# A conformer layer on one core: a table in the source sets the order of each engine's work

## The chip, the cores and the metric

The kernel runs on one core of one Trainium2 chip. The metric is the device time of one execution in microseconds. Five engines work side by side, each through its own queue of instructions in order: PE (TensorE), ACT (ScalarE), DVE (VectorE), POOL (GpSimd) and SP (SyncE, here for transfers). They wait for one another by semaphores alone.

## The reference

Two sequences of 4000 tokens, 144 features, 4 heads of 36. All data is bfloat16.

```python
h = _layernorm(x);  h = _silu(h @ w_ff1a) @ w_ff1b;  x = x + 0.5 * h
q, k, v = heads(_layernorm(x) @ w_qkv)
p = softmax(q @ k.T * Dh ** -0.5);  x = x + (p @ v) @ w_o
h = _layernorm(x) @ w_pw1;  h = h[..., :D] * _sigmoid(h[..., D:])
c = depthwise_conv(h, dw)                 # 5 taps along the tokens
x = x + _silu(c) @ w_pw2
h = _layernorm(x);  h = _silu(h @ w_ff2a) @ w_ff2b;  x = x + 0.5 * h
return _layernorm(x)
```

The hidden width of the feed-forward parts is 576. The scores are 4000 x 4000 for each head and sequence; they are the bulk of the work.

## The kernel before, in words

The tokens are cut into 16 chunks of 500 (`CH`), eight for each sequence. The keys are cut into tiles of 64 (`KT_ROWS`), 62 whole ones and one of 32. One step of attention takes one chunk of queries and one tile of keys, all four heads:

- *Scores*: four matmuls of 64 x 64 tiles on PE write two PSUM banks (PS<-QT,KT in the profile).
- *Exp*: one ACT instruction over both banks, 128 x 1000, gives the probabilities (PT<-PS). One step in about six has its exp on DVE instead: five instructions that build it from bit patterns (`dve_tile`).
- *Values*: four matmuls (PS<-PT,VA) add probabilities times values into two banks that are kept for a whole chunk.

Six PSUM banks go round among scores and everything else. The everything else is the work of a chunk before its attention (`ff1`, `pre2`: layer norm, transposes, feed-forward with tanh on ACT, projections) and after it (`epilogue`, `post1`, `post2`: division, output projection, gated convolution, second feed-forward, store). It is woven into the attention steps. In the loop a layer norm takes its statistics on DVE (ST<-X) and the rest on POOL (RS and XN), then eight transposes on PE and a copy on DVE.

No loop of the chip's program stands in the source. A planner runs when the kernel is built. `Rec.op` records each instruction with the tiles that it reads (`r`) and writes (`w`), and gives it a planned start and end from costs in the source, among them 0.095 us when PE changes from one kind of matmul to another (`SWITCH`). `Sched` holds one thread for each piece of work and `pick` takes the next piece by planned times, tables of settings for stretches of 21 steps (`POLICY`) and hand-set offsets. The order in which pieces are recorded is the order in which each engine gets them. `Rec.finish` then derives the waits: for each instruction, the latest one on every other queue that it depends on, unless an earlier wait covers it. `replay` writes the instructions out, all at one line, so that all rows of the profile carry that line; the tiles tell them apart.

In the same engine a write after a read or after a write needs no wait in this kernel (`not raw` in `finish`), because the queue is in order; a read after a write does, but on PE.

Of the kernel before, what the change touches and what calls it, by code (L numbers as in the profile page):

```python
# [44 lines left out]


class Op:
    __slots__ = ("eng", "name", "a", "k", "idx", "deps", "clock", "inc", "waits", "cnt", "q", "done", "t0", "t1", "kind")


class Rec:
# [4 lines left out]
    LAT = dict(pe=0.165, act=0.12, dve=0.083, pool=0.1, sp=2.0)  # L56
    SEM = dict(pe=0.053, dve=0.036, act=0.045, pool=0.08, sp=0.1)
    SWITCH = 0.095

    def __init__(self, nc):  # L60
        self.nc = nc
        self.ops = []
        self.n = {}
        self.hist = {}
        self.free = {e: 1.0 for e in self.ENGS}
        self.kind = None
        self.last = 0.0
        self.filler = None
        self.filling = False

    def op(self, eng, name, *a, r=(), w=(), q=None, cost=0.1, kind=None, lat=None, **k):
        o = Op()
        o.eng, o.name, o.a, o.k, o.q = eng, name, a, k, q
        o.deps, o.inc, o.cnt = [], False, 0
        lane = eng if q is None else "q:" + q
        for key in r:
            h = self.hist.setdefault(key, ([], []))
            o.deps += [(d, True) for d in h[0]]
            h[1].append(o)
        for key in w:  # L80
            h = self.hist.setdefault(key, ([], []))
# [24 lines left out]
        o.t0, o.kind = start, kind  # L106
        o.done = start + cost + ((self.LAT[eng] if q is None else 2.0) if lat is None else lat)
        self.last = o.done
        self.ops.append(o)
        return o  # L110

    def ready(self, key, eng):
        h = self.hist.get(key)
        return max([o.done for o in h[0]], default=0.0) + self.SEM[eng] if h else 0.0

    def finish(self, group_qs=()):
        eng_clock = {e: {} for e in self.ENGS}
        for o in self.ops:
            clk = eng_clock[o.eng]
            need = {}  # L120
            for d, raw in o.deps:
                lane = d.eng if d.q is None else "q:" + d.q
                if d.q is None and d.eng == o.eng and (d.eng == "pe" or not raw):
                    continue
                if clk.get(lane, -1) >= d.idx:
                    continue
                if lane not in need or need[lane].idx < d.idx:
                    need[lane] = d
            keep = []
            for lane, d in need.items():  # L130
                if any(l2 != lane and d2.clock.get(lane, -1) >= d.idx for l2, d2 in need.items()):
                    continue
                keep.append((lane, d))
            new = dict(clk)
            for lane, d in keep:
                d.inc = True
                for l2, v in d.clock.items():
                    if new.get(l2, -1) < v:
                        new[l2] = v
                if new.get(lane, -1) < d.idx:  # L140
                    new[lane] = d.idx
            o.waits = keep
            eng_clock[o.eng] = new
            o.clock = new
        self.sems = {}
        cnt = {}
        for o in self.ops:
            lane = o.eng if o.q is None else "q:" + o.q
            if o.q is not None:
                cnt[lane] = cnt.get(lane, 0) + 16  # L150
                o.inc = True
            elif o.inc:
# [87 lines left out]
class Req:  # L240
    __slots__ = ("eng", "slots", "kids", "cond", "dur", "kind", "hold")
# [17 lines left out]
class Sched:  # L259
# [26 lines left out]
        return kids  # L286

    def advance(self, th, item):
        self.cur = th
        n0 = len(self.R.ops)  # L290
        self.stepped = False
        try:
            th.req = th.gen.send(item)
        except StopIteration:
            th.live = False
            self.threads.remove(th)
        new = self.R.ops[n0:]
        if new:
            th.ready = max(th.ready, max(o.done for o in new))
# [24 lines left out]
def bass_standalone__conformer_family_zipformer__speech_kernel(  # L324
# [24 lines left out]
    R = Rec(nc)  # L349
# [165 lines left out]
    RD = sb("RD", [2, NB, 2], F32)  # L515
    AN = sb("AN", [NAN, NB, D])
# [765 lines left out]
    SAVE = QT[:, 1, T:T + 4 * CH * NQ].bitcast(F32).rearrange("p (c k n) -> p c k n", c=NQ, k=2)  # L1282
# [338 lines left out]
    while n_s[0] < NIT or eq or pend or live_dve[0]:  # L1621
        seg[0] = max(seg[0], n_s[0] // SEG)
        if mode["front"] and len(kv_done) == CPB:
            mode["front"] = False
            front[:] = [0.0, n_s[0]]
            S.add(setup_dw())
            for par in range(NPRE):
                S.add(series(pre(c) for c in range(CPB + par, NCH, NPRE)), R.last)
            for par in range(2):
                S.add(series(post2(c) for c in range(par, NCH - ALONE, 2)), R.last, rank=2)  # L1630
            for c in range(NCH - ALONE, NCH):
                S.add(post2(c), R.last, rank=2 if c < NCH - 1 else -1)
# [33 lines left out]
    while S.threads:  # L1666
        c = [(S.start_of(th), th) for th in S.threads]
# [38 lines left out]
```

## Time and profile before

| | before |
|---|---|
| median of 3 runs | 914.98 us (914.81 to 915.06) |
| profiled execution | 914.9 us, its span 913.1 us |
| granted clock | 0.999 |
| PE, matmul | 890.1 us busy, 11946 instructions |
| ACT | 872.9 us busy, 1105 |
| DVE | 802.0 us busy, 1756 |
| POOL | 277.5 us busy, 519 |

A busy time is the union of an engine's instructions from start to end. The ends of matmuls are modelled, and neighbours on ACT overlap, so a busy time is no measure of how tightly an engine's instructions follow one another. The chain of work that ended last is followed back from the end: at each step to what released the instruction, or to the one before it on its engine. "PEld" is PE's loading of weights, which runs beside its matmuls.

### The profile page before, as it was taken

How to read it: one execution, taken by the hardware profiler on the slowest of the kernel's cores; microseconds unless marked ns; L12 is line 12 of the kernel's file. 1: busy time of each engine (PE TensorE's matmuls, PEld its weight loads, DVE VectorE, ACT ScalarE, POOL GpSimd, SP SyncE). 2: the span in 40 equal slices, each digit the busy share in tenths (PEclk: the TensorE clock that was granted, in tenths of full speed). 3: DMA queues.
4: the chain of work that ended last, by engine and by line, in shares of the span. 5: the costliest groups of instructions: out<-in, count | busy, mean ns of one | idle time of the engine just before them, and what ended most of it. 6: DMA issues, size and time to landing. Idle time of an engine off the chain costs nothing.

```text
span 913.1 us, 27439 instructions
## 1 busy us (share of the span) xinstructions
PE 890.1 (97%) x11946; PEld 411.2 (45%) x11946; DVE 802.0 (88%) x1756; ACT 872.9 (96%) x1105; POOL 277.5 (30%) x519
## 2 busy tenths in 40 slices
PE   8999999999999999999999999999999999999996
PEld 7544434444444444444444444444434344444455
DVE  8988898898989999898988799897889699978987
ACT  5899999999999999999999999999999999999984
POOL 5121041145111612223415333240605050403143
PEclk9999999999999999999999999999999999999999
DMA  4000000000000000000000000000000000000000
GB/s 114 34 2 1 2 2 1 1 3 1 3 3 1 3 2 2 2 3 1 2 2 14 1 9 8 8 2 1 15 1 2 8 9 2 8 1 8 2 8 26
DMA packets 7322, 7.36 MB, mean 8 GB/s; under 512 B 2376, under 2 KB 7202, under 8 KB 7202
## 3 DMA queue, kind: packets, MB, share of 16 engines
q1 hardware_dynamic: 5786, 5.00, 1.8%
q8 instruction: 93, 1.52, 0.7%
q10 hardware_dynamic: 1416, 0.62, 0.3%
q14 instruction: 27, 0.22, 0.1%
HBM read 3.31 MB, written 2.30 MB: 6 GB/s over the span
## 4 chain that ended last, share of the span: by engine, by line
ACT 51%; PE 43%; DVE 4%; issue 1%; DMA 0%; POOL 0%; POOLq 0%; DVEq 0%
ACT PT L170 46%; PE PS L170 43%; ACT TH L170 5%; DVE HT L170 1%; DVE PT L170 1%; DVE ST L170 1%; DMA X<-in_x_dram 0%; DVE X L170 0%; DVE XN L170 0%; DVE QT L170 0%; POOL RS L170 0%; DVE XT L170 0%; DVE RS L170 0%; DVE SW L170 0%; DVE VA L170 0%
## 5 line engine op out<-in xcount | busy, mean ns | idle before, releaser
L170 ACT ACTIVATE PT<-PS 128x1000 bf16<-128x1000 f32 (+1 forms) x841 | 777.2, 1050 | 8.3 <-PE PS L170 5.9
L170 PE MATMUL PS<-QT,KT 64*64 64x500 bf16 x3968 | 415.6, 383 | 8.6 <-ACT PT L170 5.6
L170 PE MATMUL PS<-PT,VA 64*37 64x500 bf16 x4636 | 396.1, 373 | 1.9 <-DVE QT L170 1.4
L170 DVE TENSOR_SCALAR PT<-PS 128x500 int16<-128x500 f32 x334 | 222.4, 671 | 31.5 <-PE PS L170 29.5
L170 PEld LDWEIGHTS PS<-QT,KT 64*64 64x64 bf16 x3968 | 123.8, 104 | 195.7 <-ACT PT L170 112.5
L170 PEld LDWEIGHTS PS<-PT,VA 64*37 64x37 bf16 x4636 | 132.1, 95 | 111.3 <-issue 26.7
L170 POOL TENSOR_SCALAR RS<-ST 125x4 f32<-125x4 f32 x112 | 36.6, 327 | 471.0 <-DVE ST L170 465.8
L170 DVE TENSOR_SCALAR PT<-PT 128x1000 uint16<-128x1000 uint16 x334 | 134.7, 416 | 1.3
L170 POOL TENSOR_SCALAR XN<-X,RS 125x144 bf16<-125x144 bf16 x224 | 131.8, 599 | 5.8
L170 POOL TENSOR_TENSOR RS<-RS,NHALF 125x4 f32<-125x4 f32 (+2 forms) x101 | 94.1, 936 | 101.6 <-DVE RS L170 96.9
L170 DVE TENSOR_TENSOR PT<-PT 128x1000 bf16<-128x1000 bf16 x167 | 113.0, 681 | 1.5
L170 ACT ACTIVATE TH<-PS 128x500 bf16<-128x500 f32 (+3 forms) x198 | 104.3, 552 | 6.7 <-PE PS L170 5.6
L170 DVE SCALAR_TENSOR_TENSOR HT<-TH,PS 128x500 bf16<-128x500 bf16 (+1 forms) x135 | 80.6, 616 | 25.1 <-ACT TH L170 24.4
L170 PE MATMUL PS<-XT,WA 72*128 72x500 bf16 (+2 forms) x280 | 74.3, 360 | 0.6 <-DVE VA L170 0.3
L170 DVE SCALAR_TENSOR_TENSOR X<-PS,X 125x288 bf16<-125x288 f32 x128 | 57.4, 452 | 14.8 <-PE PS L170 13.1
L170 DVE BATCH_NORM_STATS2 ST<-X 125x6 f32<-125x288 bf16 (+1 forms) x160 | 65.8, 447 | 1.0 <-DMA X<-in_x_dram 0.8
L170 PE MATMUL PS<-WB,HT 128*125 128x144 bf16 (+1 forms) x640 | 52.7, 230 | 0.3 <-DVE HT L170 0.3
L170 PEld LDWEIGHTS PS<-WB,HT 128*125 128x125 bf16 (+1 forms) x640 | 44.3, 136 | 14.8 <-issue 3.8
L170 PE MATMUL PS<-IDENT,XN 125*72 125x125 bf16 x512 | 42.4, 221 | 1.5 <-DVE XN L170 0.9
L170 DVE COPY XT<-PS 72x1000 bf16<-72x1000 bf16 (+2 forms) x65 | 39.9, 617 | 3.3 <-PE PS L170 2.5
L170 PEld LDWEIGHTS PS<-IDENT,XN 125*72 125x72 bf16 x512 | 31.5, 112 | 20.2 <-issue 12.6
L170 PE MATMUL PS<-U,DG 128*128 128x250 bf16 (+5 forms) x204 | 34.3, 265 | 0.1
(86 smaller groups left out, 560.6 us busy)
## 6 DMA issues: line engine op xcount, KB each, us to landing
X<-in_x_dram SPq DMA_DIRECT2D x16, 140.6 KB
out_dram<-XN SPq DMA_DIRECT2D x14, 140.6 KB
WA<-in_w_ff1a_dram ACTq DMA_DIRECT2D x1, 144.0 KB
WB<-in_w_ff1b_dram ACTq DMA_DIRECT2D x1, 144.0 KB, 2.6
WA<-in_w_ff2a_dram SPq DMA_DIRECT2D x1, 144.0 KB
WB<-in_w_ff2b_dram SPq DMA_DIRECT2D x1, 144.0 KB
out_dram<-XN SPq DMA_DIRECT2D x2, 70.3 KB
WQKV<-in_w_qkv_dram ACTq DMA_DIRECT2D x1, 121.5 KB
```

Of the source, the lines that this page charges most:

```text
L170: ins = getattr(eng, o.name)(*o.a, **o.k)
```

## The change

The planner runs as before and records the same instructions with the same tiles, buffers and costs. Each recorded instruction now also carries a step number, `step`, which goes up by one with every piece that the planner takes. The instructions of one engine with one step number are a block. After planning, `reorder` permutes the blocks of each engine by a table in the source: one letter for each block, P for a block that stays, other letters for so many places forward or back. Then it lays the five queues into one list that respects every dependency, numbers the instructions anew, and `finish` derives the waits from that.

The dependencies get a third state. A hazard within one engine (a write after a read on the tiles in `LATE`, or with a memset) is marked `None`; `finish` skips only those marked `False`, so it may now wait for its own engine there.

```diff
+ALPHABET = '!#$%&()*+,-./0123456789:;<=>?@ABCDEFGHIJKLMNOPQRSTUVWXYZ[]^_`abcdefghijklmnopqrstuvwxyz{|}~'
+ORDER = {
+    "pe": (
+        "PPPPPPQOPPPPPPPQOPPPQQQQLPPPPQOPRPNRPNQQNPPPWOfNNNcMQMPMINPNLNNOMOMNNPTPNOOPPPPRPNPPROORRUMMPNRTMNRO"
...
+    "act": (
+        "PPPPPPPPPPPQRNOPPPPPPPPQOPPPPPPPPPROQNPPPPQOPPPPPPQOPQOPPPPRORNOPPPPPPPPPPPPPPPPPQQNPPPQOQOPPPPPPPPP"
...
+    "sp": (
+        "PPPPPPPQOPRPN"
+    ),
+}
...
+    LATE = ("MV", "RS", "NM", "VE", "RD", "AN", "XN", "SAVE")
...
         for key in w:
             h = self.hist.setdefault(key, ([], []))
-            o.deps += [(d, False) for d in h[0] + h[1] if d is not o]
+            late = key[0] in self.LATE
+            for d in h[0] + h[1]:
+                if d is not o:
+                    hazard = late and d in h[1] or "memset" in (name, d.name)
+                    o.deps.append((d, None if hazard else False))
...
+    def reorder(self, table):
+        lines = {}
+        for e in self.ENGS:
+            blocks = {}
+            for o in self.ops:
+                if o.eng == e:
+                    blocks.setdefault(o.step, []).append(o)
+            shift = [ALPHABET.index(c) - 45 for c in table[e]]
+            blocks = list(blocks.values())
+            shift += [0] * (len(blocks) - len(shift))
+            at = [None] * len(blocks)
+            for i, blk in enumerate(blocks):
+                assert at[i + shift[i]] is None
+                at[i + shift[i]] = blk
+            lines[e] = [o for blk in at for o in blk]
+        out, seen, pos = [], set(), {e: 0 for e in self.ENGS}
...
-                if d.q is None and d.eng == o.eng and (d.eng == "pe" or not raw):
+                if d.q is None and d.eng == o.eng and (d.eng == "pe" or raw is False):
                     continue
...
     def advance(self, th, item):
+        self.R.step += 1
...
         t, k, v = pick()
+        R.step += 1
...
     R.stats = stats
+    R.reorder(ORDER)
     R.finish(group_qs=("w0", "w1", "w2", "w3"))
```

More of the change, by code (lines that the diff above doesn't have):

```diff
@@ L32 @@
 EXP_BIAS = 127.0 * 128 - 76.4453125
+ALPHABET = '!#$%&()*+,-./0123456789:;<=>?@ABCDEFGHIJKLMNOPQRSTUVWXYZ[]^_`abcdefghijklmnopqrstuvwxyz{|}~'
+ORDER = {
+    "pe": (
+        "PPPPPPQOPPPPPPPQOPPPQQQQLPPPPQOPRPNRPNQQNPPPWOfNNNcMQMPMINPNLNNOMOMNNPTPNOOPPPPRPNPPROORRUMMPNRTMNRO"
+        "RPRPRRGRMOQRSQSQYIPY[GPZR[IR[GRZRY[SABBQVRUU?AEFTKPRRLMPPQRROUQJNOOPPSOPQMPPPPPPPPPQRRMNPPQSPMQNQOSO"
+        "ORNOPPPPPQQNROOPQOPSPNRNOQOPPPPPPPPPPPPPPPPPPPPPPPPPPTOPNOQOTOPNVNOVNPMMOOPQOTOPSMPMQOPPQOPQOPPPPPPP"
+        "PPPROOTOTPMMRNTPMORRMWPLUPVLOVQUHQHVQITQIMMPPPPPRORPMPQOPPPRRNNQOPRTQNLOPQQNPRPNQQNRPRPUPJOOOPQRNOQQ"
+        "NQQRMQNPPUPNSVMMUPKMNQQMQOPSPNRNOQOTOSPMMQOQQNPQQNPSOOOPPPPPPPPPQQNPQOPQQNROOPPPPPPQOQOPPSOOOPPPPPPP"
+        "PPPQOPROOSSNNRMTNOORNTNOORNTRMNSMPNSOPNTOPNQQQLQRNOQRNTNUNOSLNNQQRRLQMQQQMQOQOPPPUOPPPLQXNOOPPPPKPRS"
+        "QMRLRNQSMORNWNPPQLPRTKPRSKRSSJRURISTISPSTHTHSPSJRSSHSQJRRSIRSKPSKSNSMNRNVPQQKRRRRIRJRRRLRRRJRRKRMRRM"
+        "RM[QMPQXKOOOJXNLQQQKTTTINKRRSJRXKQQQJXOJPQLVOLPQLUMTOORRJQSPIQNQUNPPRLNSSNSMMOSSNNSPLQRMQRMQRRLQRLRR"
+        "MQRRRJWRPJPUKTMULMMSOMQRRLSPLQRRLSPLRRMSPLRRRLWQKPPQKUPLPRRLSQRJQRKSPMQRMSPMQQRLSQMQVLPPQUKRLOMPPQOR"
+        "SSSMKMPQQNUOOOOOWOOOOPPMUVNNNOMRNOQRNOQSPPLPPPPQQNQOPSOOQQMPPQOPPPPPPPPPPPPPPPPQOPPPPQQNPPPPQQQMQOPP"
+        "PPPPROOROQNPPPPPPRPNPPPPPPPPPPPPPPPPPPPQOPPPPPPQOPQOPPPQOPPPPQOPPTOOOOPPSOOOPPQOPPQOPQOPSPNRPRPTQINO"
+        "PPPPPPROQUMOOPNSOORPMRPNQOPRPNQQQMPPQQNPSOOQNPQOPQOPQOPSSNNNPQOPSSNNNQQNROOQQQMQQNPQOPQQQMRPNPRRN[MO"
+        "PPMYNNNNVNLNOMVNPPPLVNUPULOKLQNQRNQRMUWMNNNNPQTLPRMQTLOPRMQSMORRMQQLPQORRNNPQQQSLOOPQOROOPROOPPQOQQN"
+        "QQQMQRNOROOSOOQNQOQQQMQQNQQRMQQMQOQQQMQQQMQSNOQRMRNQQMPQRSOLQRMQQRLQQQLRPQMRPNROOQQNROOROOQOUOTQMMMQ"
+        "RNRPMQQNPQQNROOPQQNPQQNROOPQOROOPPPPQQNPPQTNOPNRPRMOPQQNPPQQNQOQQNQQQQLROOQOQQQMQOQQQMQQQMQOPQQRMQNR"
+        "PNQORPNQQNQQQMSQRNRKOPQQNROOPQQSSLRNLQOQQNQQNQQSMOQNRPSMRNNSOOZNOOOOPPMRXNLPNTUPLLLQNPQOQQNROORPNQOQ"
+        "QQQQKQQQMPPRPQQQKQQNROQNPPPPPPPPPPPPQOQOPPPPPPPPPPQOPPPPPPPQOPPQOPQOPPPQOQOROOSOOSNOQNQOQQQMPPROOPPP"
+        "PPQQNPPSOOOPQOPPPPPPQSNOOPQOPPPQQQMRPNPPXQNNOOPNOPTQNNOXOOOPNOORNQQSLPNQQNPPPPQQQMPQQNPQOPPPPPPQOPPP"
+        "QQNRPUPPSJNNPQOPPPPPPPPPPPUOQNNQQQLQQNPPPPPPPPQQSPLOQOPRPNPQOTOPNOQOPPROQSMORNOPQOQOQOPQQNPPPQOQOQOP"
+        "QQNPQOQQNQOQOQQNQQQMROOQQNQQQMSPNOQOSOOOQOPPQOPPPQOPPPQQQQQKRSQMMPROOPQRRMNPSSNNNPPPPRRRRSQRRRGGPPPP"
+        "PPPPPPPPQQNPPPPPPPPPPPPPPPPPSOOOPPQOPPQOPPQOPPPPTPNOOQOQOPQQNPPQOPPPPPPPPPPPPPPPPPPPPPPPPPPPQQQQLQOP"
+        "PPQOROOPQOPPQORPNQOPPQOQOPQQQRLQRMQQMPQOPROOQQNPQQNRPNPPPPSOOOPPQOPPQOPRPNQORPNQQNRPNQOPPQOPPSOOOPPP"
+        "PPPPQOPPQOPQQNPSSNNNQQQMQQRMQQMQOQQNROOPPPQQQMPQVNOUNNNRMNPSPPQLQQNRPNSOPSSSNJVPPJUNNTMNRMNZPPPLPNRP"
+        "MMPPPSPNOPSOPNSPNOQOPQOQOQOPROOQQNPQTNOOOPQRNQQRLQRMQQMQQRMQNQQSMRNNPRRRRUKQJRMRRLQMRRORLOPQOPQQNPQQ"
+        "QMPPPPPPQOQQRMOPPPPRRNNPQORROMQQRMRNOQQQQLROOQQQMPPPPPPPROOPPQOPQOPPQOPQOPPQOPPQQNPQOSOOOPROOPPPQOQQ"
+        "NPPPQQNPPPPPPPPPPQOPPPPPPPPPPPPPPQOPPPQOPQQNPPPQQNUOOOOOQOQOROOQOPPPRPQQLPPPQOPQOPQQNPPQOPPPQOPTOOOO"
+        "SOOTNOOZNPXMNOULPLLLQQNRPRMOROOPVOOOOOOROQNPROQSMPRMQNQOPPPPPQOPPPPPQOPPPPPPPPRPNPQQNROOPPPPPPQQNQOP"
+        "PPPPPPPPPQOPPSSNNSMROMQQQMPPPPPPPPPPPQOQTNPNQNPQRNQRRLSMPQRRSJRRKSPKQQRLQQMQOPQQNSSNNNPQOPQOPQOPVOWN"
+        "QULQSSISQGIQQNVOSUSTKKTJJSSSSSMIRHOPQQNPROOQOQRPMPQSPPLQOSPNOROOPPPSOPNPPROOPROOPPPPPQQN"
+    ),
+    "act": (
+        "PPPPPPPPPPPQRNOPPPPPPPPQOPPPPPPPPPROQNPPPPQOPPPPPPQOPQOPPPPRORNOPPPPPPPPPPPPPPPPPQQNPPPQOQOPPPPPPPPP"
+        "PPPPPPPQOPPPPQOPPPPPPPPPPPPPPPPPPPPPPPPPPPPPPPPPPPPPPPPPPPPPPPPPPPPPQOPPPPPPPPQOPQOPPQOPQOPPPPPPPPPP"
+        "PPPPPPPPPPPPPPPPPPPPPPPPPPPPPPPPPPPPPPPPPPQOPPPPQOPROOPSOOOPPPPPPPPPPPSSNNSMOOPPPPPPRSNNOPPPPPPPPPPP"
+        "PPPPPPPPPPRRNNQQNPPPPPPPPPPPPPPPPPPPPPPPPPPPPPPPPPPPPPPROOPPPPPPPPPROOROOPPQOQOPPPPPPPPPPPPPPPPPPPPP"
+        "PPPPPPPPPPPPPPPPPPPPPPPPPPPPPPPQOPPPROOPPPPPPPPPPPPPPPPPPPPPPQOPPPPPPPPPPPPPPPPPPPPPPQOPPPPPPPPPPPPP"
+        "PPPPPPPQOPPPPPPPPPQQNPPQOPPPPPPPPPPQOPPPPPPPPPPPPPQOPPQOQOPPPPQOPPPPPPPQOPPPPPPPQOPPQOPPPPPPPPPPPROO"
+        "PPQQNPPPPPQOPPPQOPPQOPPPPPPPPPPPPPPPPPPPPPPPPPPPPPPPPPPPPPPPPPPPPPROOPPPPPPPPPPPPPPPPPPPPPPPQOPPPPPP"
+        "PPPPPPPPPPPPPPPPPPPPPQOPPPPPPPPQOPPQOPPPPPQQNPPPPPQOPPPQOPPPPPQOPPPPPPPPPPPPPPPPPPPPPPPPPPPPPPPPPPPP"
+        "PPPPPPPPPPPQOPPPPPPPPPPQOPPPPPPPPPPPPPPPPPPPPPPPPPPPPPPPPPPRPNPPPQRNOPPPPPTOOOOPQOPPPPPPPPPPPPPPPPPP"
+        "PQOPQOPPPPPPPPPPQOPPPPPPPPPPPPPPPPPPPPPPPPPPPPPPPPPPPPPPPPPPPROOPQOPPPPPQOPPQOPPPPPPPQOPPPQOPPPPPPPP"
+        "PPPPPPPPPPPPPPPPPPPPPPQOPPPPPPPPPPPPPROOROOPQOPPPPPPPPPPPPPPPPPPQQNPPQQQMPPQOPPQOQQQQQQJPQO"
+    ),
+    "dve": (
+        "PPQOPPQOPPPROOcOOOR`MMMNQMMMPMMZOMTPPHUQRLTRPWRBOTEOMNPSOOOQOPQQQSQKQMWRPNLOOOPPPPPTOOOQNPPPVPPQQTQQ"
+        "TTFPGRRRNQRGQNPUPRUNKMXNYMOQOKOQJNPPR[NNOYNZMMMMMMQQKRKRNOPQOPPPQOQQNPQOQSNOOPQOPPPPPPPPPPPPPPPQRRRR"
+        "KRKQNRPNPTPPPTPTOOSOPQRPQQQQQQQQSPSS5RSQRTJSSESSKRJ^PPJOOOOOOOQNNQOPQOPPPPPROQNQOPPPPPPQOQOQOPPTRSMR"
+        "LQKPPPPPQQNQOPPPPPPPPPPPPPQOPPPPPPPPPPQOQOQOPQOSQNNRVNNPN`NNOOOPNZNNNNNNNNOOQOPPPPQQQMPQOROSNRNQMPPP"
+        "PPPPPPQQNPPPPPPPPPSPNOROOQOPPPPPPPSOOOPTPPSLPSPKSNORNORPNSPNSNOSNROMPPPPPRPNROOQOROQQMQOPQOQORPNROOR"
+        "OQQQLPPPQOPPQOPQOPSOPNQOPQQNPQOPPPPPRPSMPNROORPNPRPNQOQQN[OPNQNNPNOPNPPPROOPPPQOPPPPPPPPPPPPPPPPPPPP"
+        "PPPPPPPQOPPPPPPPPPPQOPPPQOPPPPPPPPPPPPQQNPPPPPPQOQRPSPKOPPPPPQOPQOPPPPPPPQOPPPQOQOQOPPPPPPPPPQQNPPQO"
+        "PPUOOOTOTLNNRNOSOPSPLRNQNPPPPQRNOPPPPPPPPPPPPPPPPPPPPPRRRMQQKPSOTOMOQNPPPPPPPPPPROQNPQOPPPQOPPPPPPPP"
+        "PPYOOOOOOOOORTRMMNPPPPPPPPPPQOQOPPPPPPPPPQOQOPQQRMQQQQQQSHPQMPPQOPQQQMPQQNROUNOOOOPQOPPPPPPPPQOUOPNO"
+        "OPTOQRMMPPPPPPPPPPPPPPPPPPPPPPPPPPPPVPQMPPLPQQQMPPPPPPQOPPQOPPPPPPQOPPPPQOPPPPPPPQOQOPQOPSPNRNOQQNQR"
+        "NOPSOPNoOOOOOOOOOOOOOOOOOOOOOPNOOOPNPNQOPPPPPPPPQOPROOROOSPROQKPPPPPPPPPPRPRMQQQQKPPQOPQQNPPPPPPPPPP"
+        "PPPQOPPPPPPPPPPPPPQQNPPQOPPP_OOOOROQLPLPNPNPWORNNNPNPPPPPPQOPPPPPPPPSORORLOPPQORPNPQOPQQQMQOPPPPPPPQ"
+        "QQMPPPQOPQOQRNQNPQOPPPPPPPQOQOPPQQQRPKPPQQNPQQNPRPQMPPPPPPPPPPQOPPPPPROQNPRPNROOQOPQOQQNPQOPQORPQQLR"
+        "RNQMPPSPNOPPTPNPQQLQQNPPPPPPPPPPPPPPQOQOPPPPQOPPPQOPPPPQOQOPPPPPPQOUOPNRNQMPPROOPPPPPPPPPPPPPPPPPPPQ"
+        "QRPQQQIPPROOPROQNQOPPPQQNPPQOPPPPPPPPPPPPROQNPRPQMQOPPPPPPPPPPPPPPPPPPQOPQOPPPPQQQMPRORPRPKPPPPPPPPR"
+        "OQQQLPPRPNPPPPPPPPPPPPPQOPPPPP^ROSLPLPLOOOOOROOQTTPLMNPQOPQRTOPROISOOOWPQORPNQHQOPTOSOTLMOORPNQOPQOP"
+        "PPPPPPPPPQQQM"
+    ),
+    "pool": (
+        "PQQQRPQQRPQSQOQQQQQQRPQQQRPQQQQQQQQQRPQQQRP%QOYOOOOOOSNORPQQIPPSQNQMPQZUQQKLSTJSKTKUUNNOFQUPQJNOPPTR"
+        "NVMMOWPNPKORNQMPRPQMPPPPPQO"
+    ),
+    "sp": (
+        "PPPPPPPQOPRPN"
+    ),
+}
@@ L47 @@
 class Op:
-    __slots__ = ("eng", "name", "a", "k", "idx", "deps", "clock", "inc", "waits", "cnt", "q", "done", "t0", "t1", "kind")
+    __slots__ = ("eng", "name", "a", "k", "idx", "deps", "clock", "inc", "waits", "cnt", "q", "done", "t0", "t1", "kind", "step")
 class Rec:
@@ L68, in __init__ @@
         self.filler = None
+        self.step = 0
         self.filling = False
@@ L105, in op @@
         self.free[eng] = o.t1 = start + cost
-        o.t0, o.kind = start, kind
+        o.t0, o.kind, o.step = start, kind, self.step
         o.done = start + cost + ((self.LAT[eng] if q is None else 2.0) if lat is None else lat)
@@ L114, in ready @@
         return max([o.done for o in h[0]], default=0.0) + self.SEM[eng] if h else 0.0
+    def reorder(self, table):
[14 more added lines that the diff above has]
+        out, seen, pos = [], set(), {e: 0 for e in self.ENGS}
+        while len(out) < len(self.ops):
+            n = len(out)
+            for e in self.ENGS:
+                while pos[e] < len(lines[e]):
+                    o = lines[e][pos[e]]
+                    if any(id(d) not in seen for d, raw in o.deps):
+                        break
+                    seen.add(id(o))
+                    out.append(o)
+                    pos[e] += 1
+            assert len(out) > n
+        count = {}
+        for o in out:
+            lane = o.eng if o.q is None else "q:" + o.q
+            o.idx = count.get(lane, 0)
+            count[lane] = o.idx + 1
+        self.ops = out
     def finish(self, group_qs=()):
```

## The prediction

> **What bounds the kernel now.** The page comes first: the span, the busy shares and the chain that ended last.
>
> ```profile
> span 913.1 us, 27439 instructions
> PE 890.1 (97%) x11946; PEld 411.2 (45%) x11946; DVE 802.0 (88%) x1756; ACT 872.9 (96%) x1105; POOL 277.5 (30%) x519
> ACT 51%; PE 43%; DVE 4%; issue 1%; DMA 0%; POOL 0%; POOLq 0%; DVEq 0%
> ```
>
> ACT and PE hand the chain to each other; nothing else carries it. The profiled execution took 914.9 us, 1.8 us outside its span, and the median of the runs is 914.98 us, so the sum below is made against 914.9. The windows view then splits the span into front, attention loop and tail. Its columns are PE, PEld, DVE, ACT and POOL busy, the granted clock and the DMA.
>
> ```profile
> 0.00:60.00 60.00, 56.04 (x674) 35.19 (x675) 53.83 (x169) 44.54 (x76) 20.93 (x42) 1.00 0.20 57
> 60.00:870.00 810.00, 798.42 (x10852) 350.50 (x10851) 715.72 (x1484) 801.92 (x982) 238.22 (x447) 1.00 0.01 4
> 870.00:913.10 43.10, 35.59 (x428) 25.50 (x423) 32.48 (x105) 26.41 (x49) 18.35 (x31) 0.97 0.06 18
> ```
>
> In the loop ACT shows only 810.00 - 801.92 = 8.1 us idle. That number is too small, and the reason decides this case. Two stretches of the chain and the groups of ACT in the loop show it:
>
> ```profile
> 771.31 23.09 ACT PT L170 x26
> 513.91 0.96 ACT TH L170 x2
> ...
> L170 ACT ACTIVATE PT<-PS 128x1000 bf16<-128x1000 f32 x800 | 745.1, 1058 | 6.6 <-PE PS L170 4.2
> L170 ACT ACTIVATE TH<-PS 128x500 bf16<-128x500 f32 x116 | 71.4, 642 | 0.5 <-PE PS L170 0.2
> L170 ACT ACTIVATE TH<-PS 128x250 bf16<-128x250 f32 x22 | 10.3, 470 | 0.5 <-PE PS L170 0.5
> L170 ACT ACTIVATE PT<-PS 128x500 bf16<-128x500 f32 x15 | 10.0, 669 | 0.0
> L170 ACT ACTIVATE TH<-PS 64x125 bf16<-64x125 f32 x15 | 4.1, 275 | 0.4
> L170 ACT ACTIVATE TH<-PS 80x125 bf16<-80x125 f32 x13 | 3.8, 291 | 0.0
> L170 ACT ACTIVATE VA<-PS 128x504 bf16<-128x504 f32 x1 | 0.6, 590 | 0.1
> ```
>
> Unhindered exps follow each other every 23.09 / 26 = 0.888 us, tanhs every 0.96 / 2 = 0.48 us, although one alone reads 1058 or 642 ns: neighbours overlap, and an exp that comes late loses its overlap and still reads busy. The loop's real need is 800 x 0.888 + 116 x 0.48 + (10.3 + 10.0 + 4.1 + 3.8 + 0.6) = 710.4 + 55.7 + 28.8 = 794.9 us. So at least 810.0 - 794.9 = 15.1 us of the loop is ACT waiting. Taken from start to start, instruction by instruction against the tightest spacing of its form, my sum is 31.9 us in the loop, 9.6 us in the front and 11.3 us in the tail. That is what a new order can reach; no instruction is removed, so the work itself stays.
>
> Why ACT waits is seen where PE's rows are laid beside ACT's:
>
> ```profile
> 218.37 0.84 PE L170 MATMUL PS<-WB,HT 128*125 128x144 bf16 x10
> 219.14 0.41 PE L170 MATMUL PS<-QT,KT 64*64 64x500 bf16 x4
> ...
> 217.51 1.90 ACT L170 ACTIVATE PT<-PS 128x1000 bf16<-128x1000 f32 x2
> 219.60 1.00 ACT L170 ACTIVATE PT<-PS 128x1000 bf16<-128x1000 f32 x1 [0.19 <-PE PS L170]
> ...
> 82.37 0.82 PE L170 MATMUL PS<-PT,VA 64*37 64x500 bf16 x12
> 83.02 0.80 PE L170 MATMUL PS<-QT,KT 64*64 64x500 bf16 x10
> ...
> 83.45 1.90 ACT L170 ACTIVATE PT<-PS 128x1000 bf16<-128x1000 f32 x2 [0.33 <-PE PS L170]
> ```
>
> Ahead of the scores (PS<-QT,KT) that feed the exp at 219.60 PE ran ten matmuls of a feed-forward residual. The exps before it started at 217.51 and 0.888 later; the next could have started at 219.29. So 0.31 us is lost, of which 0.19 is shown. At 83.45 it is twelve matmuls of probabilities times values, which nobody needed yet. PE's queue is in order: the scores stood behind the wrong block.
>
> **The change, part by part.** *PE's order.* The built order keeps all 11946 matmuls; 8860 stand at another place, by 6.5 places in the mean. I matched the trace's matmuls to the plan one by one and looked where each late ACT instruction's producer stands now. At 219.60 the ten residual matmuls stand behind the scores, at 83.45 the twelve matmuls do, and nothing was put ahead of either. Over the 47 waits of over 0.2 us in the loop, the producer moved earlier against the six producers before it in 72 to 100% of each size class, by 0.27 to 0.87 us of PE work in the mean, about the size of the wait; of the 807 ACT instructions without a wait 40% moved earlier and 37% later (by over 0.05 us). The order was moved where ACT waited. If each wait shrinks by as much as its producer moved, 20 of the 31.9 us go. That is the upper bound of this term.
>
> *Changes of kind.* PE pays when it goes from attention matmuls (64-row tiles) to the others and back:
>
> ```profile
> 67.04 0.41 PE L170 MATMUL PS<-QT,KT 64*64 64x500 bf16 x4
> 67.38 0.60 PE L170 MATMUL PS<-XT,WA 72*128 72x500 bf16 x2
> 67.90 0.41 PE L170 MATMUL PS<-QT,KT 64*64 64x500 bf16 x4
> 68.14 1.01 PE L170 MATMUL PS<-PT,VA 64*37 64x500 bf16 x16
> ```
>
> Scores to values, both attention, start 0.24 us apart (67.90 to 68.14); scores to feed-forward 0.34 (67.04 to 67.38). A change costs 0.10 us. Counted in the two built orders, the kinds change 1057 times before and 941 after: 116 x 0.10 = 11.6 us less on PE. PE carries 43% of the chain, so 0.43 x 11.6 = 5.0 us of it if nothing else helped. That is the lower bound of the loop's gain where the order helps at all. Both terms pay for the same late scores, so they aren't added; I take 12 us, about the middle of 5 and 20, since some new waits must arise.
>
> *Front and tail.* In the first 60 us ACT is busy 44.54: the sources are DMA, layer norm chains on DVE, and PE blocks such as the 20 residual matmuls that now stand behind the next feed-forward tiles. By the same count 3 of the 9.6 us go; I take 2. The tail is PE's:
>
> ```profile
> 870.31 35.39 PE PS L170 x420
> ```
>
> Its chain is one long row of PE. Behind the last scores stand 354 matmuls before and 339 after, by the work on PE 0.6 us less; of the 11.3 us that ACT waits there the count takes away 3 us, but an ACT wait in the tail costs nothing while PE works on. I take 1 us.
>
> *ACT, DVE, POOL, SP.* ACT's order moves 216 of 1111 instructions by at most 6 places: no cost. DVE moves 1043 of 1756, POOL 448 of 515. POOL could block: it is one queue of layer norms, and a norm that waits for late statistics holds up all behind it.
>
> ```profile
> POOL RS L170 <- DVE ST L170: 465.8, 42, 26.3
> PEld PS L170 <- ACT PT L170: 117.4, 323, 1.1
> DVE PT L170 <- PE PS L170: 29.5, 52, 1.3
> ```
>
> In the loop POOL waits 465.8 us for DVE's statistics, so there is room of up to 26.3 us at a time. I followed each POOL row of the new order back to the DVE rows it waits for, with the times that their places have in the trace: all but one of 3638 readers on PE and DVE find it ready, that one misses by 0.05 us. So I cost POOL at nothing; if this cover were gone, a late norm would hold its eight transposes. The output stores on SP keep their order but for four instructions.
>
> *Waits.* The new reset of waits for hazards within an engine (the third state in `deps`) could add waits on an engine's own semaphore. Counted in the built plans DVE has 429 such waits for 432, POOL 118 for 116, PE none; PE's waits for others fall from 2031 to 1976. Two more on POOL lie in its 465.8 us: nothing.
>
> The sum: 12 + 2 + 1 = 15 us, 914.9 - 15 = **900 us**. With each term at its upper bound, 20 + 3 + 3 = 26 us, it is 889; with PE's changes alone, 5, it is 910.
>
> **A rule that speaks against it.** The trace has ACT busy for 801.92 of 810.00 us in the loop. The Trainium skill ("Perfetto Trace Analysis", Identifying the Most-Contended Engine) takes occupancy on ScalarE as a fair measure of how near it is to its roof; by that 99% leaves next to nothing to win. The skill's "ScalarE: Activation LUTs" (What ACT_TABLE_LOAD costs) gives an immediate ACTIVATE 186 + 0.833 N ns and an overlap of 93 ns, an estimate of 0.926 us for each of 1000 columns in a row; 800 of these alone would take 741 us and the sum above would find no hidden wait at all. The 26 exps in 23.09 us speak against both: 0.888 us.
>
> **The rivals.**
> ACT is full: the hidden part is ACT's own time, and only the 8.1 us shown as idle can be won. Half of that gives 911 us, none of it 914.9. For it: the busy share. Against it: 0.888 against a mean of 745.1 / 800 = 0.931 us busy per exp, and the row at 219.60.
>
> Slower: the scores fall behind on PE at new places. Each ACT producer's move was also counted the other way, as a new wait once it is later than the spare that the trace shows between it and its ACT instruction: some 125 places in the loop, 30 us in the sum. If these are real, 30 - 20 = 10 us are lost: 925 us. It decides where new waits outweigh the 20 us won. For it: the count. Against it: PE itself waits there, for ACT alone 117.4 us in 323 places, so a block that moves ahead often fills a hole of PE and delays nothing; the spare was counted without these holes.
>
> That the change doesn't do what it says is excluded by the built order; that it does nothing for the time goes with the first rival.
>
> **How the numbers follow.** Forecast (889 to 910): 0.77, and with it a chance of 0.05 for more than the bounds. ACT is full: 0.12, of which 0.03 stays within 0.2% (1.8 us, what a measurement can tell from no change). Slower: 0.11. Faster 0.77 + 0.09 = 0.86. The range 889 to 914 takes in the forecast and most of the first rival.
>
> **What would show it.** Right: ACT's busy time in the loop falls although its instructions are the same (mean of an exp's busy time from 0.931 towards 0.90); the rows PS<-QT,KT and PS<-WB,HT stand the other way round at the two places shown; ACT's share of the chain rises and PE's falls. The time in the front and tail moves by less than 4 us. Wrong: ACT's busy time stays while the span does (ACT full), or the idle time of ACT behind PE and the waits of DVE PT for PE (29.5 us) grow (slower).

## The result and the profile after

The changed kernel takes **910.37 us** (median of four runs, 910.24 to 910.59) against 914.9 (914.81 to 915.06) for the kernel before: a ratio of 0.995, 95% interval 0.9938 to 0.9963. The forecast was 900. The sign was right, the size was not: 4.5 us were won of the 15 forecast. The profiled execution took 910.27 us. All times here and below are medians of fast runs; an execution in the slow state is left out.

First the page of the changed kernel (span, busy shares, chain that ended last), then its windows with the same columns and, but for the end, the same cuts as before:

```profile
span 908.5 us, 27451 instructions
PE 883.6 (97%) x11946; PEld 410.0 (45%) x11946; DVE 807.8 (89%) x1756; ACT 871.8 (96%) x1105; POOL 276.1 (30%) x519
ACT 50%; PE 43%; DVE 5%; issue 1%; DMA 0%; POOL 0%; POOLq 0%; DVEq 0%
```

```profile
0.00:60.00 60.00, 56.53 (x723) 35.88 (x723) 55.06 (x171) 47.45 (x80) 21.52 (x45) 1.00 0.20 57
60.00:870.00 810.00, 795.92 (x10838) 348.93 (x10836) 722.53 (x1485) 800.99 (x981) 237.41 (x447) 1.00 0.01 4
870.00:908.50 38.50, 31.18 (x393) 25.20 (x390) 30.22 (x101) 23.31 (x46) 17.19 (x27) 0.96 0.07 20
```

The front got fuller: in its 60 us ACT is busy 47.45 instead of 44.54 and issues 80 instructions instead of 76. The loop hardly moved: 981 ACT instructions where 982 were. ACT and PE still share the chain as before. The groups of ACT in the loop say the same of single instructions:

```profile
L284 ACT ACTIVATE PT<-PS 128x1000 bf16<-128x1000 f32 x799 | 745.0, 1061 | 5.7 <-PE PS L284 2.9
L284 ACT ACTIVATE TH<-PS 128x500 bf16<-128x500 f32 x116 | 71.4, 637 | 1.6 <-PE PS L284 1.1
```

An exp holds ACT for 745.0 / 799 = 0.932 us in the mean. Before it was 0.931, and it should have gone towards 0.90. The hidden waiting is still there.

Where the 4.5 us arose is read by laying each ACT instruction of the one trace beside the same instruction of the other and taking the difference of their starts, the lead of the changed kernel (times are those of the kernel before):

| at | 60 us | 290 | 310 | 480 | 870 | end of the span |
|---|---|---|---|---|---|---|
| lead, us | 3.15 | 3.15 | 1.8 | 0.7 | 2.7 | 4.6 |

(From 52 to 55 us it is 3.4, the value that some expectations below go by.) So the front won 3.2 us, the loop lost 0.5 on balance (nothing from 60 to 290 us, 2.4 lost from 290 to 480, 2.0 won from 480 to 870), and the tail won 2.0. The tail's window is 38.50 us long instead of 43.10 and holds 393 matmuls instead of 428.

The same matching gives each late ACT instruction, start to start as in the prediction. In the loop the sum is 32.3 us before (31.9 in the prediction, with slightly other spacings) and 32.4 after. By stretches, to 290, to 480 and to 870 us, it goes from 12.5 to 12.4, from 7.0 to 9.4 and from 12.8 to 10.6: the 2.4 lost and the 2.0 won in the lead stand beside 2.4 us more and 2.2 us less of ACT's waits. Split by place:

| ACT's waits in the loop, us | before | after |
|---|---|---|
| 122 places where ACT waited before (over 0.1 us) | 25.7 | 11.6 |
| 71 places where it waits now and did not before | 0.9 | 15.4 |

Of the 122 old waits 65 are gone altogether. **14.1 us were won at the old places and 14.5 lost at new ones.** The timelines of the changed kernel show one of each.

```profile
216.25 0.41 PE L284 MATMUL PS<-QT,KT 64*64 64x500 bf16 x4
216.59 0.84 PE L284 MATMUL PS<-WB,HT 128*125 128x144 bf16 x10
217.36 0.41 PE L284 MATMUL PS<-QT,KT 64*64 64x500 bf16 x4
214.06 6.78 ACT L284 ACTIVATE PT<-PS 128x1000 bf16<-128x1000 f32 x7
...
299.64 0.38 PE L284 MATMUL PS<-QT,KT 64*64 64x500 bf16 x4
299.86 0.38 PE L284 MATMUL PS<-PT,VA 64*37 64x500 bf16 x4
300.17 0.60 PE L284 MATMUL PS<-XT,WP 72*128 72x500 bf16 x2
300.80 0.59 ACT L284 ACTIVATE TH<-PS 128x500 bf16<-128x500 f32 x1 [0.46 <-PE PS L284]
```

At the first place the ten residual matmuls (PS<-WB,HT) now stand behind the scores that they held up. The exp that lost 0.32 us at 219.60 starts at 215.83 with no loss (it is the third of the row of seven; the exp at 83.45, which lost 0.45 us, loses nothing either). But the residual matmuls now stand directly ahead of the scores at 217.36, whose exp starts at 217.81, 0.22 us late, where it was 0.02 late before. No matmul that stood behind these scores in the old order stands ahead of them in the new one; ACT comes to them 3.65 us sooner, and PE is not ready. The row of seven doesn't show it, because an overlap lost is no idle time; it is seen in the length of the row, 6.78 us, where six spacings of 0.888 and one exp of 1.00 make 6.33 (the seventh is late too, by 0.24). At the second place 14 matmuls of scores and ten of values that stood behind the two matmuls XT,WP in the built order of before now stand ahead of them (the last four of each are shown). The two feed a tanh, and ACT waits 0.46 us shown, 0.58 from start to start, although the table has put this tanh two exps later in ACT's queue as well. In the kernel before the tanh followed the exps without a gap:

```profile
298.96 1.95 ACT L170 ACTIVATE PT<-PS 128x1000 bf16<-128x1000 f32 x2
299.75 0.60 PE L170 MATMUL PS<-XT,WP 72*128 72x500 bf16 x2
300.28 0.41 PE L170 MATMUL PS<-QT,KT 64*64 64x500 bf16 x4
300.72 0.66 ACT L170 ACTIVATE TH<-PS 128x500 bf16<-128x500 f32 x1
```

The spared PE time has a trace too. In the built orders the changes of kind in the loop fall from 996 to 887, at 0.10 us 10.9 us of PE. The waits of PE in the loop (us in total, times, longest) took it up; first those of the changed kernel, then those of the kernel before that were not shown yet:

```profile
POOL RS L284 <- DVE ST L284: 445.6, 32, 39.4
PEld PS L284 <- ACT PT L284: 122.2, 342, 1.2
PEld PS L284 <- DVE PT L284: 66.0, 218, 0.7
DVE PT L284 <- PE PS L284: 22.6, 50, 1.1
PEld PS L284 <- DVE HT L284: 19.9, 55, 0.8
PEld PS L284 <- DVE X L284: 12.8, 38, 0.5
```

```profile
PEld PS L170 <- DVE PT L170: 61.0, 212, 0.6
PEld PS L170 <- DVE HT L170: 18.1, 52, 0.5
PEld PS L170 <- DVE X L170: 10.8, 33, 0.4
```

Each of these grew: behind ACT 117.4 to 122.2, behind DVE 61.0 to 66.0, 18.1 to 19.9, 10.8 to 12.8. These sums hold weight loads that could wait without harm. Counted only where a matmul starts late against the one before it and its releaser came within 0.12 us, PE's waits rise from 32.5 to 41.2 us: behind ACT 22.9 to 24.9, behind DVE 9.6 to 16.3. That is 8.7 of the 10.9 us spared. Much of the time PE is done sooner and then stands at a result that is not there yet. The other 2.2 us don't come out as time won either, since the loop lost 0.5; where they went is not shown.

### The profile page after: what moved, and what is told of

Same layout as the page of the kernel before. It is cut to its first block, busy times and chain, and to the rows that moved or that the text cites. A ratio compares the mean times of both kernels' runs of the same rounds, so it can differ in the third digit from the quotient of the medians.

```text
span 908.5 us, 27451 instructions
## 1 busy us (share of the span) xinstructions
PE 883.6 (97%) x11946; PEld 410.0 (45%) x11946; DVE 807.8 (89%) x1756; ACT 871.8 (96%) x1105; POOL 276.1 (30%) x519
## 4 chain that ended last, share of the span: by engine, by line
ACT 50%; PE 43%; DVE 5%; issue 1%; DMA 0%; POOL 0%; POOLq 0%; DVEq 0%
ACT PT L284 45%; PE PS L284 43%; ACT TH L284 5%; DVE PT L284 2%; DVE ST L284 1%; DVE HT L284 0%; DMA X<-in_x_dram 0%; POOL RS L284 0%; DVE X L284 0%; DVE KT L284 0%; DVE QT L284 0%; DVE VA L284 0%; DVE U L284 0%; DVE XT L284 0%; DVE XN L284 0%
## 5 line engine op out<-in xcount | busy, mean ns | idle before, releaser
L284 PE MATMUL PS<-QT,KT 64*64 64x500 bf16 x3968 | 418.7, 385 | 11.8 <-ACT PT L284 7.4
L284 PE MATMUL PS<-PT,VA 64*37 64x500 bf16 x4636 | 401.7, 373 | 1.6 <-DVE QT L284 0.8
L284 DVE TENSOR_SCALAR PT<-PS 128x500 int16<-128x500 f32 x334 | 222.4, 671 | 25.0 <-PE PS L284 22.6
L284 PEld LDWEIGHTS PS<-PT,VA 64*37 64x37 bf16 x4636 | 134.1, 96 | 93.3 <-DVE PT L284 20.7
L284 POOL TENSOR_SCALAR RS<-ST 125x4 f32<-125x4 f32 x112 | 34.1, 304 | 465.3 <-DVE ST L284 459.5
L284 POOL TENSOR_TENSOR RS<-RS,NHALF 125x4 f32<-125x4 f32 (+1 forms) x101 | 95.5, 950 | 92.7 <-DVE RS L284 87.9
L284 PE MATMUL PS<-XT,WA 72*128 72x500 bf16 (+2 forms) x280 | 71.9, 359 | 0.4 <-DVE VA L284 0.2
L284 PEld LDWEIGHTS PS<-IDENT,XN 125*72 125x72 bf16 x512 | 32.0, 112 | 20.5 <-issue 10.9
L284 PEld LDWEIGHTS PS<-XT,WA 72*128 72x128 bf16 x280 | 19.7, 97 | 31.5 <-DVE HT L284 7.7
```

The source lines that it names most:

```text
L284: ins = getattr(eng, o.name)(*o.a, **o.k)
```

## The experiments

"The planner's order" is that of the kernel before. A seam is the place where the order changes from the table's to the planner's. "..." in a code cut stands for lines left out. Each kernel was timed over three rounds with the kernel before on the same chip (914.8 to 915.0 each time).

### Which part of the table brings the gain

*The front alone.* The table for the blocks that the planner takes before its planned 52 us, and the planner's order behind them.

```diff
+            at.sort(key=lambda b: (bisect([721], b[0].step), 0 if bisect([721], b[0].step) in (0,) else b[0].step))
             lines[e] = [o for blk in at for o in blk]
```

> The table's order for every block that the planner took before 52 us, the planner's own order behind it. The trace of after is 3.4 us ahead of before at 60 us and loses nothing of it up to 290 us. If the gain of the change is made in the front and kept, this kernel is 3 us faster than before: about 911.5 us. If the rest of the table has to be there to keep the lead (the loop is at its own pace and PE or ACT only waits off the lead), it is within 1 us of before, 914 to 915 us.

Measured: 912.78 us, ratio 0.9978 (0.9969 to 0.9988), between the two values expected. The lead is 2.1 us from 60 us to the end and does not change on the way. In the changed kernel it is 3.15 at that point, so 1.1 us go at the seam. So 2.0 us are the front's own. What is lost at the seam is not shown: the table put little work off past it (on PE four matmuls, 0.2 us by the planner's costs, on POOL two instructions of 1.4 us), but ACT's lead was not that of every engine, for DVE's instructions are only 1.7 us ahead there.

*The rest alone*, the same line with `in (1,)`.

> The planner's order for the first 52 us, the table's behind it: the complement. By the trace of after the loop gives nothing (lead 3.4 us at 60 us, 2.7 us at 870 us) and the tail 1.7 us: 913.5 to 914.5 us. If the prediction's sum was right for the loop and something in the front spoils it, it is 905 us or less.

Measured: 913.78 us, 0.9989 (0.9980 to 0.9999). Its lead is -0.1 us at 290 us, -2.6 at 480, -0.6 at 870, and the tail adds 1.7. The table's own stretch from 290 to 480 us loses, with no front to blame.

*The table but for 290 to 480 us* (`[3297, 5391]`, `in (0, 2)`), *but for 230 to 480 us* (`[2650, 5391]`), *and but for 52 to 480 us* (`[721, 5391]`):

> The table up to 290 us and from 480 us on, the planner's order between, where the trace of after loses 2.7 us against before. If the stretches are worth what they show by themselves, the loss isn't made: 910.4 - 2.7 = 907.7 us. If losses are passed on (a lead is eaten wherever the next narrow place is), about 910 us.

> As the choice of stretches before, but the planner's order begins at 230 us, where the lead of after is largest (3.5 to 4.0 us), and ends at 480 us. If the lead is a plain sum over stretches, 3.5 + 2.0 + 1.7 = 7.2 us: 907.6 us. If the seam costs what it gains, 909.6 us as before.

> The table for the first 52 us (2.1 us ahead at the seam, by the run that had this alone) and from 480 us on (there it gains 2.0 us up to 870 us and 1.7 us in the tail), the planner's order between. If stretches cut where little work is put off add up: 914.9 - 5.8 = 909.1 us. If the seams cost more, 910 us or above.

Measured: 909.6 (ratio 0.9944, 0.9929 to 0.9959), 909.96 (0.9947, 0.9930 to 0.9963) and **909.3** (0.9940, 0.9924 to 0.9956). The last, the table at both ends and the planner's order in the middle, is the fastest of these: its runs (908.98 to 909.68) lie 1.1 us below those of the changed kernel. That is less than the 0.2% that tells a difference, so what it shows is that the table's order from 52 to 480 us is worth nothing. The seams cost the other two what they won: in the second the lead is 3.7 us ahead of the seam (at 225 us) and 1.3 behind it.

### Can single engines take the table?

*PE alone by the table*, then *all but DVE*, then *all but POOL and SP*; the rest in the planner's order. Where the five queues so cut can't be laid into one list, the nearest ready instruction of an engine other than PE jumps ahead (33 jumps of at most four places, then 25, then one).

```diff
+            if e not in ('pe',):
+                at = blocks
...
```

> PE by the table; ACT, DVE, POOL and SP in the planner's order, but for 33 places where that order and PE's would wait for each other for ever (one instruction of DVE or ACT comes up to four places earlier there). If the gain is PE's order alone, as the prediction's terms have it: 910 to 912 us. If the orders of DVE and POOL that came with it carry the gain, PE's blocks now come ahead of data that isn't there: slower than before, 918 us or more.

> PE, ACT, POOL and SP by the table, DVE in the planner's order (25 instructions jump ahead where the two would wait for ever). PE alone by the table cost 190 us. If that was DVE's order, most of it is here again: over 1000 us. If it was POOL's, this one is within 10 us of after.

> PE, ACT and DVE by the table, POOL and SP in the planner's order (one instruction jumps). If POOL's norms come too late for PE's new order, over 950 us here; if POOL has room, as the prediction said (it waits 465.8 us for statistics), within 1 us of after, 910 us.

Measured: 1099.34 us (ratio 1.204, 1.1961 to 1.212), 1038.22 (1.1356, 1.1335 to 1.1376) and 932.64 (1.0197, 1.0182 to 1.0212). The last is neither of the two values expected for it. The waits of the three over the whole span, in that order:

```profile
PEld PS L293 <- DVE PT L293: 141.5, 257, 3.6
ACT TH L293 <- PE PS L293: 95.7, 90, 4.7
ACT PT L293 <- PE PS L293: 82.0, 101, 4.1
```

```profile
PEld PS L293 <- DVE PT L293: 153.6, 269, 3.6
ACT PT L293 <- PE PS L293: 82.3, 112, 4.1
```

```profile
PEld PS L293 <- POOL XN L293: 12.2, 5, 5.8
ACT PT L293 <- PE PS L293: 12.0, 17, 5.9
```

With DVE in the planner's order PE waits up to 3.6 us for one of DVE's probabilities, and ACT's exps wait 82.3 us behind it. With POOL in the planner's order a few norms are late by up to 5.8 us each. So the moves on DVE and POOL are what lets PE's order run: 128 us are lost without DVE's (1038.22 - 910.37) and 22 without POOL's and SP's. Whether they bring anything by themselves was not run. The jumps are part of these prices, and so is PE's granted clock, which was 0.929, 0.963 and 0.983 in the three profiles against 0.998 in the changed kernel; PE's busy time is 928.8 us in the second against 883.6. So these are prices of a misfit, not the bare worth of an order.

### Can the late scores be moved one by one?

*The kernel before, with 66 of its late score and tanh blocks moved one to three blocks ahead on PE.* By the count of the prediction the moves are worth 14.2 us.

```diff
+FIX = [
+    (872, 869), (965, 961), (1106, 1099), (1190, 1187), (1407, 1406), (1514, 1511), (1536, 1533), (1556, 1553),
...
+            if e not in ():
+                at = blocks
+            for a, b in FIX if e == "pe" else ():
+                row = [blk[0].step for blk in at]
+                at.insert(row.index(b), at.pop(row.index(a)))
```

> The planner's order on all engines, but at 66 places of the loop where ACT waited over 0.1 us for PE in the trace of before, the block that ACT waited for goes one to three blocks further ahead, past blocks that ACT wasn't waiting for. By the trace these moves are worth up to 14.2 us. If placing late scores is what counts and what is pushed back has slack, most of it comes: 903 to 906 us. If a wait that is taken away comes back at another place (as in the loop of after: old places 25.7 to 11.6 us, new ones 0.9 to 15.4), 913 us or more.

Measured: 916.22 us, 1.0015 (1.0006 to 1.0025): 1.4 us slower, just clear of no change. The waits at the 122 old places fall from 25.7 to 13.9 us, almost as counted. At 52 new places they rise from 1.2 to 12.9. Two of those, in its timeline of ACT:

```profile
218.40 1.00 ACT L302 ACTIVATE PT<-PS 128x1000 bf16<-128x1000 f32 x1 [0.17 <-PE PS L302]
...
223.72 1.90 ACT L302 ACTIVATE PT<-PS 128x1000 bf16<-128x1000 f32 x2 [0.24 <-PE PS L302]
```

Start to start they are 0.30 and 0.36 us, where the same exps of the kernel before lost nothing. They stand beside two waits that the moves did take away, 0.48 us at 214.00 and 0.38 at 222.73 of the kernel before. The changes of kind number 1049 against 1057, so this kernel has the table's kind of move with little of its saving on PE.

*The changed kernel with 53 more such moves*, worth 12.3 us by the same count:

> The changed kernel with the same repair at the 53 places of its own trace, worth up to 12.3 us there. If the waits of after are misplaced blocks, 900 to 904 us. If the loop keeps its sum of waits whatever is moved, 909 us or more.

Measured: 914.01 us, 0.9990 (0.9981 to 1.0), 3.6 us slower than the changed kernel. Old places 26.0 to 19.0, 41 new ones 1.2 to 10.7. The pattern is the same from either start: a wait taken away by order comes back at another place. (This kernel also has 963 changes of kind where the changed kernel has 941, so a part of the 3.6 us can be PE's.)

*The changed kernel with 20 swaps on ACT*: a tanh that waits lets the next exp, which is ready, go first. Worth 4.7 us if ACT's waiting is all that counts.

> The changed kernel; at the 20 places of its trace where ACT waited over 0.1 us for a tanh's matmuls while the exp behind it in ACT's queue had its scores, the two change places on ACT. By the trace that is worth up to 4.7 us, and each swapped tanh comes an exp (0.88 us) later. If ACT's waits can be taken away by order at all, 906 to 908 us. If they come back at other places, as with the score blocks, 909.5 us or more.

Measured: 916.42 us, 1.0019 (1.0008 to 1.0029), 6 us slower than the changed kernel. Two rows of its waits in the loop, and behind them the same two of the changed kernel:

```profile
PEld PS L294 <- DVE U L294: 13.6, 21, 1.4
DVE U L294 <- ACT TH L294: 11.3, 11, 1.8
```

```profile
PEld PS L284 <- DVE U L284: 5.7, 17, 0.5
DVE U L284 <- ACT TH L284: 3.1, 5, 1.3
```

The later tanh holds up a DVE instruction (U), and that holds up PE: start to start, PE's waits behind DVE go from 16.3 to 27.9 us. Nor does ACT keep what the swaps won: its waits at the swapped tanhs only fall from 5.0 to 2.7 us, and over the loop they rise by about 6 us.

### What is a microsecond of each engine worth?

Three kinds of work were thinned, each in both kernels, with the order kept.

*PE:* two of the five matmuls of each feed-forward residual, 256 in all, are left out (the residual lacks these terms). From the rows at 218.37 and 219.14 ten of them take 0.77 us with one change of kind, so about 0.067 each and 17.2 in all. 184 of them stand in the loop, 12.3 us.

```diff
...
+                if len(terms[i]) == 5 and t in (1, 2):
+                    R.left_out.add(id(o))
```

> The kernel before with its order, but two of the five terms of every feed-forward residual are left out: 256 of the 640 matmuls of PS<-WB,HT, at 0.0625 us each 16 us of PE's time, about 14 of it in the loop. It takes PE work away as the 116 spared changes of kind do (11.6 us), but moves nothing. If PE's time in the loop is worth what the prediction said (43%), it gains 6 to 7 us: 908 us. If PE only waits the time off (nothing comes of spared PE work in the loop), 914 us. By the places where ACT waits behind such a block in the trace (34 of them) about 6 us can go.

> The changed kernel with the same 256 matmuls of the feed-forward residuals left out. On the order of before that took 6.0 us off (914.83 to 908.81). If PE's time is worth as much in the table's order, so that the 10.6 us of spared changes of kind are a gain of some 4.5 us in the loop which the moves then eat up: 904.3 us. If the table's order made the loop depend less on PE (and so lost the value of the spared changes there): 907 us or more.

*ACT:* from step 41 on each exp leaves out the last 10 of 500 columns of both banks.

```diff
+    FULL = 40
...
+        m = CH if n < FULL else CH - 10
+        op("act", "activation", PT[:, pt, :, 0:m], PSV[:, lo:hi + 1, 0:m], ACT.Exp, bias=0.0,
```

> The kernel before with its order; from the 41st step on each exp on ACT leaves out the last 10 of 500 columns of both banks: 20 columns of 1000, 17 ns each by the 0.884 us that 1000 columns take, 13 us of ACT's work. PE's 14 us were worth 6.0 us here. If ACT carries the other half of the path, as the chain says (51%), about 6.5 us are gained: 908.4 us.

> The changed kernel with the same 13 us of ACT's work left out. PE's 14 us were worth only 3.0 us here. If the table's order made ACT and the banks that it frees the pace of the loop (what PE spares is waited off at ACT), ACT's work is worth more than on the order of before: 9 us or more, 901 us or less. If the table's order is late on transfers of results among all engines, so that neither engine's work counts for as much, 5 us or less are gained: 905.5 us or more.

*DVE:* the last of the five instructions of the exp on DVE is left out in 41 of 167 steps.

```diff
...
+        R.tiles += 1
+        if R.tiles % 4 == 0:
+            R.left_out.add(id(o))
```

> The kernel before with its order; in 41 of the 167 steps whose exp is made on DVE the last of the five instructions (0.326 us each by the spacing of starts) is left out, 13 us of DVE's work. In the loop of before PE waits 9.6 us for DVE and 22.9 us for ACT. If DVE is off the path there, under 1.5 us are gained: 913.5 us or more.

> The changed kernel with the same 13 us of DVE's work left out. In its loop PE waits 16.3 us for DVE (9.6 before) and 24.9 us for ACT (22.9 before). If DVE is what became late when PE's order was packed, it gains clearly more here than on the order of before, 3 us or more: 907 us or less. If PE's spared time only went into waits for ACT and the banks that ACT frees, it gains as little as there: 909 us or more.

What was taken away is seen in the traces. Unhindered, 24 exps in the chain of the kernel before take 21.53 us, in that with shorter exps 21.12:

```profile
95.55 21.53 ACT PT L170 x24
```

```profile
95.33 21.12 ACT PT L170 x24
```

That is 0.017 us for each of 785, 13.4 us. On DVE the group of 334 instructions of 134.7 us has become one of 293 and 118.8. That is 15.9 us of busy time; neighbours overlap on DVE too, and by the spacing of starts, 0.326 us, the 41 are 13.4 us:

```profile
L170 DVE TENSOR_SCALAR PT<-PT 128x1000 uint16<-128x1000 uint16 x334 | 134.7, 416 | 1.3
```

```profile
L179 DVE TENSOR_SCALAR PT<-PT 128x1000 uint16<-128x1000 uint16 x293 | 118.8, 416 | 1.5
```

Measured, with the gain over the kernel that was thinned (914.9 and 910.37):

| thinned | kernel before | gain, of it per us | changed kernel | gain, of it per us |
|---|---|---|---|---|
| PE, 17.2 us | 908.81 (ratio 0.9934, 0.9920 to 0.9949) | 6.0, 0.35 | 907.35 (0.9917, 0.9902 to 0.9932) | 3.0, 0.18 |
| ACT, 13.4 us | 908.76 (0.9933, 0.9916 to 0.9950) | 6.2, 0.46 | 904.81 (0.9890, 0.9875 to 0.9905) | 5.6, 0.42 |
| DVE, 13.4 us | 915.58 (1.0008, 0.9999 to 1.0018) | -0.7, 0 | 909.91 (0.9945, 0.9928 to 0.9963) | 0.5, 0.03 |

In the loop alone, by the leads at 60 and 870 us, over the kernel that was thinned, leaving out PE's matmuls won 4.6 of 12.3 us before (0.37) and 2.6 in the changed kernel (0.21), shortening ACT's exps 6.0 of 13.4 us in either (0.45 and 0.44).

Before, PE and ACT together set 0.35 + 0.46 = 0.81 of the time. In the changed kernel they set 0.18 + 0.42 = 0.60. DVE's work, as far as this one instruction stands for it, sets none in either. The ACT run of the changed kernel lies between its two expected values: ACT's share has not grown, so it has not taken over what PE lost. A microsecond less work on PE is worth half of what it was. What is left, a fifth before and two fifths after, I take to be in the hand-offs: PE standing at results that come late by order, not by work. That is an inference; no run shows it. The chains of the pair thinned on PE, before and changed, point the same way, PE's share falling more in the second:

```profile
ACT 53%; PE 39%; DVE 6%; issue 1%; DMA 0%; POOL 0%; POOLq 0%; DVEq 0%
```

```profile
ACT 59%; PE 32%; DVE 7%; issue 1%; DMA 0%; POOL 0%; POOLq 0%; DVEq 0%
```

## Why the prediction was right and where it failed

**What bounds the kernel: right, and tested.** PE and ACT hand the chain to each other, with 43% for PE and 51% for ACT; the thinned kernels give 0.35 of PE's work back (0.37 in the loop) and 0.46 of ACT's, somewhat below these shares. ACT's busy share of 99% did hide waiting: 13.4 us less of ACT's work brought 6.2, not 13. The first rival (ACT is full) also named 911 us, and the time came out near it, but by luck: ACT waits 32 us in the loop of the changed kernel, and PE's work still has a price.

**The recovery at the old places: right in kind, too large.** "If each wait shrinks by as much as its producer moved, 20 of the 31.9 us go." At the old places 14.1 went. Both rows that the prediction named stand the other way round, and both waits are gone.

**The loop's 12 us: the step that failed.** "I take 12 us, about the middle of 5 and 20, since some new waits must arise" put new waits in as a rounding of the recovery. They are a term of their own, of the same size: 14.5 us in 71 places. The slower rival had counted them, 30 us in some 125 places, twice too many, and was set aside with the reason that "a block that moves ahead often fills a hole of PE and delays nothing". Its own form of the sum, recovery less new waits, gives 14.1 - 14.5 = -0.4 us for the loop, and the loop measured -0.5. The single moves show why no such reason was to be had: with 66 of them, or 53, the sum of ACT's waits did not fall (old places -11.8 and new ones +11.7; -7.0 and +9.5). On PE's queue a block that goes ahead puts off what it passes, as at 300.80; and where nothing was put in front of a block, as at 217.36, ACT reaches it sooner and waits there. These two ways are seen at places, not counted over all 71.

**The lower bound of 5: no bound.** "0.43 x 11.6 = 5.0 us" holds only while PE's spared time stays on the chain. The 11.6 us are those of the whole kernel (10.9 in the loop), and the share of a chain is no price: by thinning, a microsecond of PE in the loop was worth 0.37 before and 0.21 in the changed kernel, and 8.7 of the 10.9 us became waits of PE for ACT and DVE. The term doesn't show by stretches either: 47 fewer changes of kind from 60 to 290 us went with no gain, 15 fewer from 290 to 480 with 2.4 us lost, 47 fewer from 480 to 870 with 2.0 won. That 47 x 0.10 x 0.43 also makes 2.0 for the last is chance, for the price isn't even along the loop: in the kernel before, the thinned PE won 0.56, 0.25 and 0.25 us a microsecond in the three stretches.

**Front and tail: under-sized, and most of the gain.** The front was put at 2 (at most 3) and won 3.2, of which 2.1 stay if the planner's order follows. The tail was put at 1 (at most 3) and won 2.0. Together they are 5.1 us, more than the whole.

**ACT, POOL, waits: right; DVE: open.** POOL still waits 445.6 us for statistics, and its cover was real. DVE, put at nothing without a count of its own, is the more important one: its order carries PE's, and of the 8.7 us by which PE's waits grew 6.7 are behind DVE, though leaving out the one DVE instruction won nothing.

**The signs named in advance.** ACT's busy time in the loop was to fall with the loop's gain; it went from 801.92 to 800.99, which was the early sign of the miss. ACT's share of the chain was to rise and PE's to fall; they went from 51 to 50% and stayed at 43%. Front and tail were to move by less than 4 us; they moved by 5.1 together. For the slower case the waits of DVE PT for PE were to grow from 29.5 us; they fell to 22.6, and those in the other direction, PE for DVE, grew. The sign was read off the wrong side of the hand-off.

Two small readings are off as well: the 6.5 places are the mean over all 11946 matmuls (8.8 over the 8860 that moved), and the 116 changes of kind spared hold 109 in the loop.

Left open: which hand-offs carry the missing two fifths in the changed kernel, what a seam costs its microsecond or two for, and why the new waits outweigh the old ones between 290 and 480 us and not behind it, though the changes of kind fall in both (218 to 203, 463 to 416).

## What to carry to other kernels

A new order of the same instructions has two terms, the waits it takes away and the waits it makes, and both are to be counted place by place and set against each other before either is discounted; here they were 14.1 and 14.5 us. In this kernel the order's gain lay at the ramp and at the end; the steady loop, in which two engines feed each other, gave 2.0 us in its second half and lost more ahead of it. How much a microsecond of an engine is worth is measured by thinning its work a little, and measured again after a change, since the change can move it.

## What was not expected of the hardware's behaviour

The engines' orders belong together far more tightly than their loads suggest: of DVE's work 13.4 us could be thinned for nothing, and yet the kernel took 128 us more, at a granted clock of 0.963, when DVE's order did not fit PE's. The Trainium skill ("Perfetto Trace Analysis", Identifying the Most-Contended Engine) takes ScalarE's occupancy as a fair measure of how near its roof it is. This trace does not agree: before the change ACT read busy for 801.92 of 810.00 us although 32.3 us of the loop, start to start, were waiting, and a microsecond less of its work was worth 0.46.
